# Second MoE of a fused attention and two-MoE kernel: output groups and x steps placed behind a weight pair's seven products

## The chip, the core and the metric

The kernel runs on one core of a Trainium2 chip. The metric is the device time of one execution in microseconds (us). The kernel before has a median of 1036.16 us over 3 runs (1035.74 to 1036.51).

The engines are named as the profile names them: PE is TensorE (matrix products, results go to PSUM), PEld its weight loads, DVE is VectorE, ACT is ScalarE, POOL is GpSimd and SP is SyncE, which here only issues DMAs.

## What is computed

A causal attention with a forget gate, and behind it two feed-forward blocks on 2304 tokens of 512 values. The change touches the second block alone:

```python
def _moe2_ref(x, w_gate, w_val, w_out):          # x 2304x512, w_gate and w_val 512x1536, w_out 1536x512
    gate = 1.0 / (1.0 + np.exp(-(x @ w_gate)))
    val = x @ w_val
    return (gate * val @ w_out).astype(np.float32)
```

## The kernel before, in words

Every float32 product is made of three matmuls on operands split into a high and a low part: high by high, high by low, low by high (function `three`, lines 552 to 558).

The second MoE (class `Moe2`) cuts the tokens into 3 tiles of 768. Within a tile it walks over 12 units: unit r = 0, 2, 4, ... multiplies a pair of column blocks of w_gate, unit r = 1, 3, 5, ... the same pair of w_val, so there are 36 units, k = 0 to 35. One unit computes a 2 by 2 block product with **seven products** instead of eight (a scheme in Strassen's manner), each of 6 matmuls with 384 columns. I call them P1 to P7, in their order in `hidden`: A11, A12, S2, S1, S3, S4, A22.

The seven products share **two PSUM banks**, a and b: P1, P3, P5, P7 go to a, and P2, P4, P6 to b; P3, P5 and P6 add to what the bank already holds. So between two products on one bank the bank has to be read out, and only one product on the other bank lies between. The readers are, each 384 columns wide:

- after P1: ACT copies a to p1 (line 850); after P2: DVE adds b and p1 to c0 (line 853)
- after P3: ACT copies a to u2 (line 856); after P4: ACT copies b to p5 (line 859)
- after P5: ACT copies a to u3 (line 864), and DVE adds a and p5 to c3 (line 865): two readers of one bank, on two engines
- after P6: DVE adds b and u2 to c1 (line 868); after P7: DVE adds a and u3 to c2 (line 876)

In an even unit ACT then applies the sigmoid to c0 and c1 (line 870), and to c2 and c3 in the next unit (line 878). In an odd unit DVE multiplies by the gate (lines 872 and 880), and `high` (line 889, ACT) and `low` (line 895, DVE) split the result.

Beside its seven products a unit carries the **output groups** of a hidden block that was finished two units earlier: six groups (`piece`, lines 914 to 916) of 3 matmuls with 512 columns, which accumulate into six PSUM banks of their own. In the kernel before, the groups lie among the products: one behind each of P3, P4, P5 and P6, and two behind P7 (the calls of `between`). Units 0 and 1 have no output groups. At the end of a tile the six accumulators leave through `leave` (line 925: a copy on DVE or ACT; line 926: a DMA issued by SP); this falls into the unit r = 1 of the next tile and behind the last unit.

In the units r = 2 to 11 of the first two tiles a **step** prepares one tenth of the next tile's x: its DMAs on ACT's queue (line 794), or a split by ACT (line 788) and DVE (line 789) with some subtractions on DVE (lines 799 to 809). It stands behind P4, between the copies to p5 and to u3. Steps for the first tile run in the first MoE, those of the third tile's units don't exist.

The order is written out by hand: the program's order on each engine is the order of the lines. At the end of a unit SP gets the loads of later weights (`load_out`, line 763, and `load`, lines 753 and 758).

Of the kernel before, what the change touches and what calls it, by code (L numbers as in the profile page):

```python
# [551 lines left out]
def three(nc, ps, terms, start, stop, **how):  # L552

    n = len(terms)
    for i, (ah, al, bh, bl) in enumerate(terms):
        nc.tensor.matmul(ps, ah, bh, start=start and i == 0, stop=False, **how)  # L556
        nc.tensor.matmul(ps, ah, bl, start=False, stop=False, **how)  # L557
        nc.tensor.matmul(ps, al, bh, start=False, stop=stop and i == n - 1, **how)  # L558


def block(w, i):
    return w[:, 128 * i:128 * i + 128]


class Moe1:
# [12 lines left out]
    def hidden(self, u, pieces):  # L578
        nc, ch, W = self.nc, self.chain, self.W
        t, fc = divmod(u, self.FC)  # L580
        N = self.TILES[t][1]
        (wh, wl), (xh, xl) = self.W.done[f"wi{fc}"], self.x.parts[t]
        ph = self.ps.tile([128, 512], F32, tag="s", bufs=2, name=f"h{u}")[:, 0:N]
        three(nc, ph, [(block(wh, c), block(wl, c), xh[:, c], xl[:, c]) for c in range(4)], True, True)
        g = ch.tile([128, 512], F32, tag="L", name=f"L{u}", bufs=2)[:, 0:N]
        nc.scalar.activation(g, ph, AF.Softplus)  # L586
        self.mid[u] = g
        self.parts(u)
        W.tick(pieces)
# [38 lines left out]
    def unit(self, u, pieces):  # L628

        t, fc = divmod(u, self.FC)  # L630
        k = fc - 5
        if self.TILES[t][1] < 512:
            k = fc // 2 if fc % 4 in (0, 3) else -1
        if 0 <= k < 8 and t + 1 < self.NT:
            self.x.step(t + 1, k)
        self.hidden(u, pieces)
# [18 lines left out]
class Sums:  # L655
# [11 lines left out]
    def add(self, lane, sums, names, srcs):  # L667

        for n in names:
            self.d[n] = self.dr.tile([4 if sums else 1, 2, 128, 512], F32, name="sd_%s%d" % n)  # L670
        self.lanes[lane].append((sums, names, srcs))
# [52 lines left out]
class Moe2:  # L724
# [95 lines left out]
        return w  # L820


    def hidden(self, k, fill):
        t, r = divmod(k, 2 * self.J)
        nc, gate = self.nc, r % 2 == 0
        m = self.TILES[t][1] // 2
        A, B = self.weights(k), self.tokens(t)
        C = [self.chain("GV"[r % 2] + "01"[f], k) for f in range(2)]
        G = [self.chain("G" + "01"[f], k) for f in range(2)]
        p1, u2, p5, u3 = (self.chain(n, k)[:, 0:m] for n in ("p1", "u2", "p5", "u3"))  # L830
        c = lambda i: C[i // 2][:, m * (i % 2):m * (i % 2) + m]
        if k == 0:
            self.banks = [self.ps.tile([128, 512], F32, tag="s", bufs=2, name=f"z{i}") for i in range(2)]
        a, b = (self.banks[(k + i) % 2][:, 0:m] for i in range(2))

        def product(ps, w, x, start):
            terms = [(block(A[w][0], kk), block(A[w][1], kk), *B[x][kk]) for kk in range(2)]
            three(nc, ps, terms, start, True, skip_group_check=True)

        def issue(fs):  # L840
            while fs:
                fs.pop(0)()

        def between(n=1):
            for _ in range(n):
                if fill:
                    fill.pop(0)()
        add = nc.vector.tensor_add
        product(a, "A11", "x11", True)
        nc.scalar.copy(p1, a)  # L850
        issue(self.early)
        product(b, "A12", "x21", True)
        add(c(0), b, p1)
        issue(self.late)
        product(a, "S2", "T2", False)
        nc.scalar.copy(u2, a)  # L856
        between()
        product(b, "S1", "T1", True)
        nc.scalar.copy(p5, b)
        if t + 1 < self.NT and r >= 2:  # L860
            self.step(t + 1, r - 2)
        between()
        product(a, "S3", "T3", False)
        nc.scalar.copy(u3, a)  # L864
        add(c(3), a, p5)  # L865
        between()
        product(b, "S4", "x22", False)
        add(c(1), b, u2)
        if gate:
            nc.scalar.activation(C[0], C[0], AF.Sigmoid)  # L870
        else:
            nc.vector.tensor_mul(C[0], C[0], G[0])  # L872
            self.high(k // 2, 0, C[0], m)
        between()
        product(a, "A22", "T4", True)
        add(c(2), a, u3)
        if gate:
            self.early.append(lambda: nc.scalar.activation(C[1], C[1], AF.Sigmoid))
        else:
            nc.vector.tensor_mul(C[1], C[1], G[1])  # L880
            self.low(k // 2, 0, C[0], m)
            self.early.append(lambda: self.high(k // 2, 1, C[1], m))
            self.late.append(lambda: self.low(k // 2, 1, C[1], m))
        between(2)

    def high(self, i, f, s, m):
        h = [self.chain(f"gh{x}", i)[:, 0:m] for x in range(2)]
# [38 lines left out]
        nc.sync.dma_start(self.out[o:o + 128, :], z)  # L926

    def unit(self, k, fill):
        self.hidden(k, fill)
        for f in fill:  # L930
            f()
        self.load_out(k + 2)
        self.load()
# [28 lines left out]
def kernel(ctx: ExitStack, tc, q, k, v, f, w_in, w_out, w_gate, w_val, w2_out, out):  # L962
# [60 lines left out]
    for i, (n, j, w) in enumerate(gv):  # L1023
        lane = i % 3 // 2
        unit = lambda: S.add(lane, True, [(n, j)], [w[2 * j], w[2 * j + 1]])
        pair = lambda f: S.add(lane, False, [("w2", f), ("w2", f + 1)], [w2_out[f], w2_out[f + 1]])
        if lane and i < 9:
            pair(4 * (i // 3))
        unit()
        if lane and i < 9:  # L1030
            pair(4 * (i // 3) + 2)
# [118 lines left out]
```

## Time and profile before

| what | value |
|---|---|
| median of 3 runs | 1036.16 us |
| the profiled execution's own time | 1036.21 us |
| its span, first to last instruction | 1034.4 us |
| PE busy in it | 1009.9 us (98%) |
| DVE, ACT, POOL busy | 620.9 (60%), 503.1 (49%), 153.5 (15%) |
| the second MoE's units | 609.5 to 1022 us of the span |

A row of the timeline has the start in us from the span's first instruction, the duration in us, the engine, the line of the code, the operation, out<-in by the program's names and the shape; in brackets stands the idle time of the engine just before it and what ended that. Matmuls are pipelined: one of 384 columns is shown with 0.33 us, yet the next starts 0.17 us after it. What a matmul costs is therefore read from the starts of two neighbours, not from its duration.

The code names p1 and u2 `p` and `u` in the trace; p5 lies in a buffer shown as `bh`, u3 in one shown as `bl`.

### The profile page before, as it was taken

What the parts mean: (1) busy time and instruction counts of PE and PEld (TensorE: products, weight loads), DVE (VectorE), ACT (ScalarE), POOL (GpSimd) and SP (SyncE); (2) the same over time, 40 slices, a digit from 0 to 9 for tenths busy, and PEclk for the clock granted to TensorE, in tenths of its full rate; (3) what the DMA queues carried; (4) which work ended last, traced back from release to release, by engine and by line L of the source; (5) the groups of instructions that cost most, each with busy time, mean ns of one, the idle gap of its engine ahead of it and who ended that gap; (6) DMA issues with size and microseconds to landing.
All of it is one profiled execution on the core that took longest, in us unless ns stands there. A gap on an engine that the chain in (4) does not pass through costs nothing.

```text
span 1034.4 us, 15839 instructions
## 1 busy us (share of the span) xinstructions
PE 1009.9 (98%) x5584; PEld 883.5 (85%) x5584; DVE 620.9 (60%) x1238; ACT 503.1 (49%) x1069; POOL 153.5 (15%) x158
## 2 busy tenths in 40 slices
PE   5999999989999999999999999999999999999998
PEld 4788877768888889988888889999999999999996
DVE  4899999978955666646626743545444434443333
ACT  4889988866544445444334544333333333333332
POOL 8566777540000000000000000000000000000000
PEclk9999999999999999999999999999999999999999
DMA  5354554444635656736525786666667676666631
GB/s 146 111 144 137 157 160 125 138 150 176 217 122 191 221 196 233 255 95 241 195 100 208 252 316 226 208 215 198 224 228 265 203 246 219 207 234 216 223 123 61
DMA packets 114698, 196.07 MB, mean 190 GB/s; under 512 B 14702, under 2 KB 38398, under 8 KB 114620
## 3 DMA queue, kind: packets, MB, share of 16 engines
q1 hardware_dynamic: 112684, 189.98, 55.0%
q10 hardware_dynamic: 1936, 5.09, 1.4%
q8 instruction: 44, 0.72, 0.3%
q14 instruction: 34, 0.28, 0.1%
HBM read 149.19 MB, written 45.83 MB: 189 GB/s over the span
## 4 chain that ended last, share of the span: by engine, by line
PE 91%; DVE 3%; ACT 2%; DMA 1%; issue 1%; SPq 1%; POOL 0%; ACTq 0%; DVEq 0%; POOLq 0%
PE z L558 8%; PE z L557 8%; PE z L556 8%; PE h L556 6%; PE h L557 6%; PE h L558 6%; PE s L223 4%; PE x L330 4%; PE t L254 4%; PE oY L556 2%; PE oY L557 2%; PE oY L558 2%; PE o L557 2%; PE o L558 2%; PE o L556 2%; PE oX L556 2%
## 5 line engine op out<-in xcount | busy, mean ns | idle before, releaser
L557 PE MATMUL z<-three,three 128*128 128x384 f32 x456 | 154.2, 338 | 0.0
L558 PE MATMUL z<-three,three 128*128 128x384 f32 x456 | 153.7, 337 | 0.0
L556 PE MATMUL z<-three,three 128*128 128x384 f32 x456 | 153.0, 336 | 0.5 <-ACT u L856 0.2
L586 ACT ACTIVATE L<-h 128x512 f32<-128x512 f32 (+1 forms) x80 | 44.3, 553 | 152.4 <-PE h L558 152.2
L598 DVE TENSOR_TENSOR gl<-L,gh 128x512 fp32r<-128x512 f32 (+1 forms) x80 | 51.1, 638 | 108.8 <-ACT gh L597 108.6
L556 PEld LDWEIGHTS z<-three,three 128*128 128x128 f32 x456 | 85.6, 188 | 8.1 <-DVE raw L865 0.9
L557 PEld LDWEIGHTS z<-three,three 128*128 128x128 f32 x456 | 85.4, 187 | 6.2
L235 ACT ACTIVATE P<-P,m 128x128 f32<-128x128 f32 (+3 forms) x144 | 83.3, 582 | 10.7 <-DVE m L230 10.3
L558 PEld LDWEIGHTS z<-three,three 128*128 128x128 f32 x456 | 85.7, 188 | 0.0
L230 DVE CUSTOM_DVE_ANT_0 P<-s,mask 128x256 f32<-128x256 f32 (+3 forms) x144 | 70.7, 516 | 12.3 <-PE s L223 7.5
L280 DVE TENSOR_TENSOR PTl<-t,PTh 128x512 fp32r<-128x512 f32 (+2 forms) x112 | 66.9, 619 | 5.1 <-ACT PTh L276 4.9
L254 PE MATMUL t<-ident,P 128*128 128x128 f32 x400 | 61.4, 287 | 7.3 <-DVE PTl L280 5.7
L865 DVE TENSOR_TENSOR raw<-z,bh 128x384 f32<-128x384 f32 x36 | 20.0, 556 | 78.0 <-ACT bl L864 78.0
L276 ACT CAST PTh<-t 128x512 fp32r<-128x512 f32 (+2 forms) x112 | 56.4, 537 | 18.3 <-PE t L254 17.8
L254 PEld LDWEIGHTS t<-ident,P 128*128 128x128 f32 x400 | 44.6, 144 | 21.5 <-DVE PTl L280 7.2
L889 ACT CAST gh<-raw 128x384 fp32r<-128x384 f32 x72 | 33.5, 514 | 50.1 <-DVE raw L872 49.2
L330 PE MATMUL x<-PTh,V 128*128 128x256 f32 (+2 forms) x224 | 56.3, 311 | 0.0
L850 ACT COPY p<-z 128x384 f32<-128x384 f32 x36 | 17.3, 481 | 76.5 <-PE z L558 76.5
L330 PE MATMUL x<-PTl,V 128*128 128x256 f32 (+2 forms) x224 | 54.3, 293 | 0.0
L700 DVE TENSOR_TENSOR l<-fw,sh 128x512 fp32r<-128x512 f32 x60 | 40.7, 687 | 16.2 <-ACT sh L699 14.9
L597 ACT CAST gh<-L 128x512 fp32r<-128x512 f32 (+1 forms) x80 | 46.3, 579 | 2.5
L699 ACT CAST sh<-fw 128x512 fp32r<-128x512 f32 x60 | 35.8, 619 | 19.4 <-DMA sd_g<-sh 9.9
(284 smaller groups left out, 2630.3 us busy)
## 6 DMA issues: line engine op xcount, KB each, us to landing
three<-sd_g SPq DMA_DIRECT2D x126, 256.0 KB
three<-sd_v SPq DMA_DIRECT2D x126, 256.0 KB
two<-sd_w SPq DMA_DIRECT2D x36, 256.0 KB
raw_wi<-in_moe_w_in_dram SPq DMA_DIRECT2D x16, 512.0 KB
raw_wo<-in_moe_w_out_dram SPq DMA_DIRECT2D x16, 512.0 KB
fraw<-in_moe_w_gate_dram SPq DMA_DIRECT2D x12, 512.0 KB
fraw<-in_moe_w_out_dram SPq DMA_DIRECT2D x12, 512.0 KB
sd_g<-sh SPq DMA_DIRECT2D x24, 256.0 KB
```

The costliest lines, as they stand in the source:

```text
L230: self.nc.vector.tensor_tensor_reduce(P, src, mask, -0.125, 3e38, op0=ALU.add, op1=ALU.min, accum_out=R["m"][:, t:t + 1])
L235: self.nc.scalar.activation(P, P, AF.Exp, bias=R["m"][:, t:t + 1], scale=-1.0, accum_out=R["sum"][:, t:t + 1])
L254: nc.tensor.transpose(ps[:, 128 * n:128 * n + 128], R["P"][:, o:o + 128], self.ident)
L276: self.nc.scalar.copy(d, s)
L280: self.nc.vector.tensor_sub(l, s, h)
L330: nc.tensor.matmul(R["acc%d" % h][:, o:o + n], v, t[:, col:col + n], start=j == 0 and w == 0, stop=j == 1 and w == 1)
L556: nc.tensor.matmul(ps, ah, bh, start=start and i == 0, stop=False, **how)
L557: nc.tensor.matmul(ps, ah, bl, start=False, stop=False, **how)
L558: nc.tensor.matmul(ps, al, bh, start=False, stop=stop and i == n - 1, **how)
L586: nc.scalar.activation(g, ph, AF.Softplus)
L597: nc.scalar.copy(gh, s)
L598: nc.vector.tensor_sub(gl, s, gh)
```

## The change

`hidden` loses its argument `fill` and with it the calls of `between`: P1 to P7 now follow each other in the program with their readers alone. The x step moves from behind P4 to the end of `hidden`. The six output groups are emitted by `unit`, behind `hidden`. Nothing is added or removed, and the order of P1 to P7, of their readers and of the groups among themselves stays.

```diff
-    def hidden(self, k, fill):
+    def hidden(self, k):
...
-        def between(n=1):
-            for _ in range(n):
-                if fill:
-                    fill.pop(0)()
...
         product(a, "S2", "T2", False)
         nc.scalar.copy(u2, a)
-        between()
         product(b, "S1", "T1", True)
         nc.scalar.copy(p5, b)
-        if t + 1 < self.NT and r >= 2:
-            self.step(t + 1, r - 2)
-        between()
         product(a, "S3", "T3", False)
         nc.scalar.copy(u3, a)
         add(c(3), a, p5)
-        between()
         product(b, "S4", "x22", False)
         add(c(1), b, u2)
...
-        between()
         product(a, "A22", "T4", True)
         add(c(2), a, u3)
...
-        between(2)
+        if t + 1 < self.NT and r >= 2:
+            self.step(t + 1, r - 2)
...
     def unit(self, k, fill):
-        self.hidden(k, fill)
+        self.hidden(k)
         for f in fill:
             f()
```

## Rows read from the trace of the kernel before

**Rows 1.** The page, parts 1 and 2: busy time, and the granted clock in 40 slices

```profile
PE 1009.9 (98%) x5584; PEld 883.5 (85%) x5584; DVE 620.9 (60%) x1238; ACT 503.1 (49%) x1069; POOL 153.5 (15%) x158
PEclk9999999999999999999999999999999999999999
```

**Rows 2.** By stretch: length, busy PE, PEld, DVE, ACT, POOL, clock, DMA: unit 1; twelve units

```profile
619.97:628.27 8.30, 7.90 (x43) 7.25 (x42) 2.89 (x5) 3.22 (x7) 0.00 (x0) 1.00 0.65 223
778.44:917.08 138.64, 138.64 (x721) 128.95 (x720) 61.38 (x103) 49.86 (x95) 0.00 (x0) 1.00 0.68 229
```

**Rows 3.** Timeline of PE: unit 3's P1, first group and P4; unit 35's P1

```profile
639.82 0.33 PE L556 MATMUL z<-three,three 128*128 128x384 f32 x1
...
642.94 0.39 PE L914 MATMUL zt<-raw,gh 128*128 128x512 f32 x1
...
643.64 0.33 PE L556 MATMUL z<-three,three 128*128 128x384 f32 x1
...
1009.64 0.33 PE L556 MATMUL z<-three,three 128*128 128x384 f32 x1
```

**Rows 4.** Timeline of unit 34: P5's last matmul and its two readers

```profile
1004.56 0.33 PE L558 MATMUL z<-three,three 128*128 128x384 f32 x1
...
1004.98 0.48 ACT L864 COPY bl<-z 128x384 f32<-128x384 f32 x1 [1.28 <-PE z L558]
...
1005.50 0.56 DVE L865 TENSOR_TENSOR raw<-z,bh 128x384 f32<-128x384 f32 x1 [3.57 <-ACT bl L864]
```

**Rows 5.** Line 865's own view: what ended the idle time before it (us, times)

```profile
  ACT bl L864: 78.0, 24
```

**Rows 6.** Timeline of PE, unit 0: starts of P1, P6, P7, the next matmuls, unit 1

```profile
609.48 0.33 PE L556 MATMUL z<-three,three 128*128 128x384 f32 x1
...
614.74 0.33 PE L556 MATMUL z<-three,three 128*128 128x384 f32 x1
...
616.06 0.44 PE L556 MATMUL z<-three,three 128*128 128x384 f32 x1
...
617.21 0.39 PE L556 MATMUL oX<-gh,wo_h 128*128 128x512 f32 x1
...
619.97 0.33 PE L556 MATMUL z<-three,three 128*128 128x384 f32 x1
```

**Rows 7.** Timeline of unit 1: P6, the two readers of P5, P7, unit 2's P1

```profile
625.73 0.33 PE L556 MATMUL z<-three,three 128*128 128x384 f32 x1
...
625.98 0.48 ACT L864 COPY bl<-z 128x384 f32<-128x384 f32 x1 [1.08 <-PE z L558]
...
626.50 0.56 DVE L865 TENSOR_TENSOR raw<-z,bh 128x384 f32<-128x384 f32 x1 [3.00 <-ACT bl L864]
...
627.11 0.44 PE L556 MATMUL z<-three,three 128*128 128x384 f32 x1 [0.17 <-DVE raw L865]
...
628.27 0.33 PE L556 MATMUL z<-three,three 128*128 128x384 f32 x1
```

**Rows 8.** Timeline of PE behind the last unit: the output groups at the end

```profile
1021.42 0.40 PE L915 MATMUL zt<-three,gh 128*128 128x512 f32 x1
1022.08 0.50 PE L916 MATMUL zt<-three,gl 128*128 128x512 f32 x1 [0.26 <-DVE gl L895]
1022.41 0.40 PE L914 MATMUL zt<-three,gh 128*128 128x512 f32 x1
...
1029.46 0.39 PE L915 MATMUL zY<-two,gh 128*128 128x512 f32 x1
```

**Rows 9.** Timeline of DVE: unit 8 (c0, x step), unit 14 (last DVE leave, c0)

```profile
699.92 0.56 DVE L853 TENSOR_TENSOR bl<-z,p 128x384 f32<-128x384 f32 x1 [1.05 <-PE z L558]
...
703.96 0.96 DVE L789 TENSOR_TENSOR three<-bh,three 128x768 fp32r<-128x768 f32 x1 [2.54 <-ACT three L788]
...
768.40 0.69 DVE L925 COPY fw<-zY 128x512 f32<-128x512 f32 x1
769.24 0.56 DVE L853 TENSOR_TENSOR bl<-z,p 128x384 f32<-128x384 f32 x1 [0.15 <-PE z L558]
```

## The prediction, made before the changed kernel was run

> **What bounds the kernel now.** I read the page first: PE is busy for 98% of the span at the full granted clock, and POOL has nothing to do in the second half [rows 1]. Then the busy time by stretch: in twelve units of the second MoE PE is busy for all of 138.64 us, while DVE and ACT work for 44% and 36% of it, and the clock is at 1.00, the level of 2.4 GHz [rows 2]. So PE's stream is the bound, and the other engines count only where PE would have to wait for them. Third, the timeline of PE: from unit 3's P1 to unit 35's P1 lie 32 units in 369.82 us, **11.557 us a unit** [rows 3]. Three products one behind the other take 642.94 - 639.82 = 3.12 us, so 1.04 us a product, and an output group between two products takes 0.70 us [rows 3]. PE never stops in these units.
>
> The decisive view is the timeline around P5. Its last matmul starts at 1004.56; ACT starts the u3 copy 0.42 us later and takes 0.48 us; DVE's c3 add, which needs only the bank and the older p5, starts at 1005.50, 0.04 us behind the end of the copy, and takes 0.56 us [rows 4]. The add waited for the copy in all 24 of the 36 units in which DVE was otherwise free [rows 5]. So the two readers of bank a go one behind the other, and P7, which overwrites that bank, can start about 0.42 + 0.48 + 0.04 + 0.56 + 0.05 = 1.55 us after P5's last matmul did. Now P6 and two groups lie in between (0.17 + 1.04 + 2 x 0.70 = 2.6 us), which hides it.
>
> Units 0 and 1 have no output groups: the trace of before already holds **the order that the change makes**, seven products back to back. There PE does stop. In unit 0 P6 starts at 614.74 and P7 at 616.06, 1.32 us instead of 1.04 to 1.05; in unit 1 it is 627.11 - 625.73 = 1.38 us, and the row of P7 names line 865 as its releaser [rows 6, 7].
>
> **Part 1, the products close up.** P1 to P5 of unit 0 take 614.74 - 609.48 = 5.26 us, with no wait of any size [rows 6]; so one product is enough cover for the readers of P1 to P4, which are single (0.42 + 0.48 + 0.05 = 0.95 us for a copy on ACT, 1.03 us for an add on DVE, against 0.17 + 1.04 = 1.21 us). That cover is thin, 0.2 us. P6 up to P7 takes 1.32 us in unit 0 and 1.38 us in unit 1; I take the 1.38 us, since there the copy starts as late as in the later units (0.42 us after P5's last matmul, as in rows 4 and 7). P7 itself takes longer behind the stop: 617.21 - 616.06 = 1.15 us and 628.27 - 627.11 = 1.16 us [rows 6, 7]. Sum of the seven products: 5.26 + 1.38 + 1.16 = **7.80 us**.
>
> **Part 2, the six groups in one piece.** Eighteen matmuls of 512 columns behind a product: twelve of the first MoE's take 619.97 - 617.21 = 2.76 us [rows 6], and deep in such a run they follow at (1029.46 - 1022.41) / 31 = 0.227 us [rows 8], so 2.76 + 6 x 0.227 = **4.12 us**. That is less than six single groups (6 x 0.70 = 4.20 us); the products gain a little too where no group interrupts them, and both are in these sums.
>
> A unit becomes 7.80 + 4.12 = 11.92 us against 11.557 us: **+0.36 us in each of the 34 units with groups (2 to 35)**, +12.3 us. The banks' readers after P6 and P7 lie under the groups then, so the next unit's P1 and P2 find them done.
>
> **Part 3, the end.** Behind the last unit PE now stops for the split that the last groups need: from 1021.42 to 1022.41 pass 0.99 us for two matmuls instead of 0.45, released by line 895 on DVE [rows 8]. With four more groups (2.8 us) between P7 and these, that split is done in time: **-0.5 us**.
>
> **Part 4, the x step.** Twenty steps move. Of each, ACT's copy of 768 columns and DVE's 0.96 us subtraction [rows 9] with at most two of 384 columns behind it (0.56 us each, by the add of that width in rows 4) leave the place between p5 and u3 and come behind P7's readers. In unit 8 the step ran ahead of c3; that cost nothing, and its absence gains nothing, as c3 is tied to u3. Behind it on DVE now stands the next unit's c0, which P4 waits for. In unit 8 DVE stood idle for 1.05 us before c0 with no DVE step in the unit before [rows 9]; four groups more behind P7 add 2.8 us to that, a step takes about 2.1 us from it, so some 1.7 us remain: no cost. The step's two DMA issues (units r = 2 and r = 7) move on ACT's queue past u3 and the sigmoid; the data is used a unit later, as before. SP's loads stay behind the last group of the unit, which still ends the unit; POOL has no part in it. Cost nothing, as long as those 1.7 us hold.
>
> **Part 5, the accumulators' leaving (units 13 and 25).** The copies of line 925 now come within 4 us, and the fifth must find the buffer of the first sent out. In unit 14 DVE had only 0.15 us to spare between such a copy and c0 [rows 9]. After the change the last DVE copy ends about as close to c0. I take nothing for it; the bound is that each of the two copies ends one copy later, 0.69 us [rows 9], so 0 to +1.4 us.
>
> **Sum.** +12.3 - 0.5 = +11.8 us; of this I take 0.1 off for units 14 and 26, the first of their tiles, which like unit 0 should wait 0.06 us less. On the profiled execution's own 1036.21 us that gives **1047.9 us**; the median before is 1036.16 us, so nothing changes between the two bases. Bounds: with unit 0's shorter wait everywhere and P1 without the 0.02 us that it costs behind a long run of groups, 11.83 us or +0.27 us a unit, 34 x 0.27 - 0.5 = +8.7, 1044.9 us; with part 5's 1.4 us and a few tenths where the 0.2 us covers fail by chance, 1049.9 us.
>
> **The rivals.** *Faster: c3 is not tied to u3.* If DVE reads the bank beside ACT, P7 can start 0.42 + 0.56 + 0.05 = 1.03 us after P5's last matmul, and the cover of 1.21 us holds. A unit then takes 6.30 + 1.04 + 4.12 = 11.46 us, 0.10 us less than now: 34 x 0.10 + 0.5 = 3.9 us saved, **1032.3 us**. For it: neither reader needs the other's result. Against it: all 24 free cases, and both units without groups [rows 5 to 7]; the program's order of these two lines stays. Of the Trainium skill two pages bear on this one. "TensorE: Matmul & The Clock Gate" (Loop structure matters more than you think) recommends matmuls back to back, with the copy out of PSUM beside them and the next matmuls following at once; by it the time would be this rival's. "PSUM — Partial Sum Buffer" (PSUM bank collisions raise a hardware error) says that two engines must not touch one bank at a time, two reads included, and wants a semaphore there; by that rule the tie stays, and the 24 waits agree.
>
> *Slower still: the moved step delays c0.* If DVE's step runs into the next unit's c0 by d, P4 starts late by about d - 0.2 us. It decides once the step ends over 1.7 us later than I have it, for instance because a DMA of x lands late; then 20 units with 0.3 us each, **1054 us**. Against it: DVE's share of 44% [rows 2].
>
> *No change: the tie is there, but closing up repays it.* That needs 0.36 us a unit found elsewhere; the groups and products have no more to give than the sums hold. It would be 1036 us, or 1034.1 to 1038.3 us, the 0.2% within which a measurement of this kernel can't tell a change.
>
> **How the numbers follow.** My forecast 0.87, the faster rival 0.07, the slower one 0.04, no change 0.02. The likeliest case gives 1047.9 us; its bounds 1044.9 to 1049.9 hold over 8 in 10, and the others stay outside. Faster by over 0.2%: 0.07; within: 0.02; slower: 0.91.
>
> **What would show it.** In the changed trace each unit from 2 on should have one stop of PE, ahead of P7, released by line 865's add, with P6 to P7 at about 1.38 us; the c3 add should start within 0.05 us of u3's end; the unit should take 11.92 us, its 18 group matmuls 4.12 us; the stop behind the last unit should be gone. I am wrong if the add starts beside the copy, if P7 starts 1.04 us after P6, or if a stop ahead of P4 or of the next P1 appears.

## The result, and the profile after

| | before | after |
|---|---|---|
| median | 1036.07 us (1035.74 to 1036.51, 4 runs) | 1048.02 us (1047.70 to 1048.62, 4 runs) |
| ratio to before | | 1.0119, 95% interval 1.0106 to 1.0131 |
| profiled execution, its span | 1036.21 us, 1034.4 us | 1048.24 us, 1046.5 us |

The changed kernel is 1.2% slower; 1047.9 us was predicted. The lines of the code have moved: the copy to u3 is now line 856 (864 before), the c3 add line 857 (865), c1 859 (868), c0 849 (853), the output groups 905 to 907 (914 to 916).

The page of the changed kernel, to be held against [rows 1]; the third row is the group of the first matmuls of `three` (after the bar: busy us, mean ns; after the second bar: idle us before them, and what ended most of it), and the fourth is the same group in the kernel before:

```profile
PE 1017.3 (97%) x5584; PEld 884.1 (84%) x5584; DVE 619.1 (59%) x1238; ACT 503.1 (48%) x1069; POOL 152.8 (15%) x158
PEclk9999999989999999999999999999999999999999
L556 PE MATMUL z<-three,three 128*128 128x384 f32 x456 | 157.6, 346 | 6.4 <-DVE raw L857 6.0
...
L556 PE MATMUL z<-three,three 128*128 128x384 f32 x456 | 153.0, 336 | 0.5 <-ACT u L856 0.2
```

PE has the same 5584 matmuls. New is the idle time ahead of line 556, 6.4 us where it was 0.5, 6.0 us of it released by the c3 add. That is only half of the loss: a matmul is drawn with 0.33 us though the next could start after 0.17, so a part of each stop lies under the drawn end of the matmul before it. Again the starts of neighbours are what counts. The one slice with a clock of 8 lies at 209 to 235 us, in the attention, and is not where the time went: unit 0's P1 starts at 609.36 us, and at 609.48 us before [rows 6].

The timeline of unit 34 in the changed kernel: P5's last matmul, P6, u3, c3, P6's last matmul, P7, the first group, unit 35's P1. The first row of all is unit 3's P1:

```profile
640.22 0.33 PE L556 MATMUL z<-three,three 128*128 128x384 f32 x1
...
1015.04 0.33 PE L558 MATMUL z<-three,three 128*128 128x384 f32 x1
1015.21 0.34 PE L556 MATMUL z<-three,three 128*128 128x384 f32 x1
...
1015.47 0.48 ACT L856 COPY bl<-z 128x384 f32<-128x384 f32 x1 [0.56 <-PE z L558]
...
1015.98 0.56 DVE L857 TENSOR_TENSOR raw<-z,bh 128x384 f32<-128x384 f32 x1 [2.16 <-ACT bl L856]
...
1016.08 0.34 PE L558 MATMUL z<-three,three 128*128 128x384 f32 x1
...
1016.59 0.45 PE L556 MATMUL z<-three,three 128*128 128x384 f32 x1 [0.17 <-DVE raw L857]
...
1017.77 0.39 PE L905 MATMUL zt<-two,gh 128*128 128x512 f32 x1
...
1021.89 0.33 PE L556 MATMUL z<-three,three 128*128 128x384 f32 x1
```

Read it against [rows 4]. P5's last matmul starts at 1015.04; u3 follows 0.43 us later, c3 0.03 us behind u3's end, P7 0.05 us behind c3's end: 1016.59 - 1015.04 = 1.55 us. Between P6's first matmul and P7's lie 1.38 us instead of 1.04. P7 takes 1.18 us, the 18 group matmuls 1021.89 - 1017.77 = 4.12 us. From unit 3 to unit 35 lie (1021.89 - 640.22) / 32 = **11.927 us a unit**, against 11.557 us before [rows 3]: 0.37 us each.

The views of line 857 (what it waited for and who waited for it: us, times) and of PE's waits (engine, line, us in total, times, longest) in the changed kernel from 600 us on give the same on all units; the third fence is PE's waits in the kernel before:

```profile
  ACT bl L856: 95.1, 36
...
  PEld z L556: 17.7, 36
```

```profile
PE z L556 <- DVE raw L857: 6.0, 35, 0.2
PE z L556 <- ACT u L852: 0.2, 1, 0.2
```

```profile
PE zt L916 <- DVE gl L895: 0.3, 1, 0.3
PE z L556 <- ACT u L856: 0.2, 1, 0.2
PE z L556 <- DVE raw L865: 0.2, 1, 0.2
```

c3 waited for u3 in all 36 units (24 in [rows 5]; in the others the x step had kept DVE busy), and weight loads waited for c3 in all 36. The stop behind the last unit [rows 8], released by line 895 then, has no row any more.

### The profile page after: what moved, and what is told of

Same layout as the page of the kernel before. It is cut to its first block, busy times and chain, and to the rows that moved or that the text cites. A ratio compares the mean times of both kernels' runs of the same rounds, so it can differ in the third digit from the quotient of the medians.

```text
span 1046.5 us, 15854 instructions
## 1 busy us (share of the span) xinstructions
PE 1017.3 (97%) x5584; PEld 884.1 (84%) x5584; DVE 619.1 (59%) x1238; ACT 503.1 (48%) x1069; POOL 152.8 (15%) x158
## 4 chain that ended last, share of the span: by engine, by line
PE 89%; DVE 6%; ACT 3%; issue 1%; DMA 1%; ACTq 0%; SPq 0%; DVEq 0%
PE z L556 8%; PE z L558 7%; PE z L557 7%; PE h L557 6%; PE h L558 6%; PE h L556 6%; PE s L223 5%; PE x L330 4%; PE t L254 4%; PE oY L557 2%; PE oY L556 2%; PE oY L558 2%; PE o L557 2%; PE o L558 2%; PE o L556 2%; DVE raw L857 2%
## 5 line engine op out<-in xcount | busy, mean ns | idle before, releaser
L849 DVE TENSOR_TENSOR raw<-z,p 128x384 f32<-128x384 f32 x18 | 10.0, 558 | 88.9 <-PE z L558 88.9
```

## Experiments

The theory: the two readers of bank a after P5, on two engines, go one behind the other; this chain of 1.55 us needs more than one product as cover, and with the groups gone from between the products PE stops ahead of P7 in every unit. Rivals: the moved x step costs the time; the order itself does (long stretches of one shape); or c3 waits for something of u3's own and not for the bank's other reader.

### The step put back, the groups alone behind

```diff
         nc.scalar.copy(p5, b)
+        if t + 1 < self.NT and r >= 2:
+            self.step(t + 1, r - 2)
         product(a, "S3", "T3", False)
...
-        if t + 1 < self.NT and r >= 2:
-            self.step(t + 1, r - 2)
```

> The changed kernel with the x step put back between the copies to p5 and to u3; only the output groups lie behind the products. Theory (PE stops ahead of P7 because c3 must follow u3 on bank a): the step's DVE work now stands ahead of c3 with no group to cover it. In the units of the first two tiles where c3 came late in the trace of before (4 units with p5's start to c3's start 3.2 us, 8 units with 2.6 us), P7 moves later by 1.6 and 1.05 us: 4 x 1.6 + 8 x 1.05 = 15 us over the changed kernel, so about 1063 us (1060 to 1066), with the longer stop in these 12 units alone. Rival (the moved step is what costs the 12 us): with the step back in its place the time returns, 1036 to 1040 us.

Measured: **1067.62 us**, ratio 1.0306 (1.0292 to 1.0320). Slower still, so the moved step is not what costs; left in place it would have cost some 20 us more. The timelines of DVE and PE in unit 8 of this kernel (c3 is line 859 here), then PE's waits:

```profile
708.65 0.96 DVE L789 TENSOR_TENSOR three<-bh,three 128x768 fp32r<-128x768 f32 x1 [1.85 <-ACT three L788]
709.52 0.55 DVE L799 TENSOR_TENSOR bl<-bh 128x384 f32<-128x384 f32 x1
710.11 0.56 DVE L800 TENSOR_TENSOR bh<-bh 128x384 f32<-128x384 f32 x1
710.59 0.55 DVE L859 TENSOR_TENSOR raw<-z,bh 128x384 f32<-128x384 f32 x1
```

```profile
709.06 0.34 PE L558 MATMUL z<-three,three 128*128 128x384 f32 x1
711.20 0.45 PE L556 MATMUL z<-three,three 128*128 128x384 f32 x1 [1.80 <-DVE raw L859]
...
712.12 0.52 PE L557 MATMUL z<-three,three 128*128 128x384 f32 x1
712.43 0.52 PE L558 MATMUL z<-three,three 128*128 128x384 f32 x1
```

```profile
PE z L556 <- DVE raw L859: 20.9, 34, 1.8
```

The step's three DVE instructions stand ahead of c3 in DVE's order, and P7 starts 2.14 us after P6's last matmul instead of 0.17. That is the expected part. The result lies 1.6 us above the expected range, and the rows show why: behind the stop two matmuls of 384 columns lie 0.31 us apart, not 0.17. The busy time by stretch in this kernel (length, busy time and count of PE, PEld, DVE, ACT, POOL, then the granted clock) for unit 3, the end of unit 8 and unit 4, whose stop is shorter:

```profile
639.73:653.25 13.52, 11.72 (x61) 10.65 (x60) 6.85 (x11) 4.22 (x8) 0.00 (x0) 1.00 0.52 176
...
711.20:716.00 4.80, 4.80 (x15) 4.11 (x16) 0.96 (x2) 0.84 (x1) 0.00 (x0) 0.64 0.06 19
...
653.25:666.18 12.93, 11.73 (x61) 10.66 (x60) 4.41 (x8) 4.22 (x8) 0.00 (x0) 1.00 0.55 182
```

After the stop of unit 8 the granted clock falls to its lower level of 1.2 GHz for a while (0.64 as the mean of the stretch). Units 15 and 20 show the same (0.89 as the mean of each unit), unit 3 doesn't, though its stop is as long. These three units take 15.1 us against unit 3's 13.52 us: 3 x 1.6 = 4.8 us, which brings the expected 1063 us to 1067.8 (the profiled execution took 1066.82 us).

### The step alone moved

```diff
         nc.scalar.copy(p5, b)
-        if t + 1 < self.NT and r >= 2:
-            self.step(t + 1, r - 2)
         between()
...
         between(2)
+        if t + 1 < self.NT and r >= 2:
+            self.step(t + 1, r - 2)
```

> The kernel before with the x step alone moved behind P7's readers; the groups stay among the products. Theory: the step is off the path in either place, 1036.1 us (1035.5 to 1036.7), units of 11.55 us, c3 right behind u3 in every unit. Rival (the moved step delays the next unit's c0, or its DMAs come late): 1038 us or more, with a stop ahead of P4.

Measured: **1035.71 us**, ratio 0.9995 (0.9985 to 1.0004): no change. PE is busy for all of 360 us in this kernel's busy time by stretch, although the step now runs right up to the next unit's c0 on DVE (no idle time ahead of line 853 in the second fence):

```profile
640.00:1000.00 360.00, 360.00 (x1872) 334.60 (x1871) 152.02 (x256) 125.56 (x242) 0.00 (x0) 1.00 0.65 221
```

```profile
653.57 0.56 DVE L800 TENSOR_TENSOR bh<-bh 128x384 f32<-128x384 f32 x1
654.05 0.55 DVE L853 TENSOR_TENSOR bl<-z,p 128x384 f32<-128x384 f32 x1
```

In this order a group stands between P3 and P4 and covers c0: c0 ends at 654.60, P4 starts at 654.72, and the group starts at 654.02, where P4 would have stood without it. So the step costs nothing here, but because of the group and not because DVE had time to spare.

### One reader of the bank: c3 made from u3

```diff
         nc.scalar.copy(u3, a)
-        add(c(3), a, p5)
+        add(c(3), u3, p5)
```

> The changed kernel with c3 made from u3, the copy in SBUF of what bank a holds, and not from bank a: the same sum, but bank a has one reader after P5. Theory (the two readers one behind the other are the whole loss): P7 can start about 0.42 + 0.48 + 0.05 = 0.95 us after P5's last matmul, the cover is 1.21 us, so the stop goes: units of 11.46 us, 34 x 0.47 less than the changed kernel, about 1032 us (1031 to 1033.5), faster than both. Rival (runs of one shape, seven products and six groups at a stretch, cost by themselves, or another wait takes the place of this one): 1040 to 1048 us.

Measured: **1030.91 us**, ratio to the kernel before 0.9948 (0.9935 to 0.9960): faster than both kernels, with one word changed. The timeline of its unit 34 (P5's last matmul, u3, c3, P7) between its unit 3's and unit 35's P1:

```profile
638.00 0.33 PE L556 MATMUL z<-three,three 128*128 128x384 f32 x1
...
997.56 0.33 PE L558 MATMUL z<-three,three 128*128 128x384 f32 x1
...
997.98 0.48 ACT L856 COPY bl<-z 128x384 f32<-128x384 f32 x1 [0.56 <-PE z L558]
...
998.50 0.56 DVE L857 TENSOR_TENSOR raw<-bl,bh 128x384 f32<-128x384 f32 x1 [2.15 <-ACT bl L856]
...
998.77 0.33 PE L556 MATMUL z<-three,three 128*128 128x384 f32 x1
...
1003.93 0.33 PE L556 MATMUL z<-three,three 128*128 128x384 f32 x1
```

c3 still starts at u3's end, but now it reads `bl`, that is u3, and P7 starts while it runs: 998.77 - 997.56 = 1.21 us, the plain length of the cover. No stop of PE is left in units 3 to 35. A unit takes (1003.93 - 638.00) / 32 = 11.435 us, 0.49 us less than in the changed kernel and 0.12 us less than before. So the order as such is a small gain; the stop turned it into the loss.

### The same edit in the old order

```diff
         nc.scalar.copy(u3, a)
-        add(c(3), a, p5)
+        add(c(3), u3, p5)
         between()
```

> The kernel before with c3 made from u3 in the same way; groups and step stay where they were. Theory: a group between P5 and P6 and another between P6 and P7 hide the two readers anyway, so nothing changes: 1036.1 us (1035.4 to 1036.7). Rival (taking a read off the PSUM bank helps PE, DVE or ACT by itself, whatever the order): 1034 us or less.

Measured: **1035.73 us**, ratio 0.9995 (0.9987 to 1.0004): no change. Where the groups stand among the products, the second reader is hidden anyway, and units take 11.55 us as before. The edit is worth something only where the cover is short: units 0 and 1, which have no groups, lose their stop and take 10.07 and 7.82 us instead of 10.49 and 8.30 us. Unit 2 gives 0.3 us of that back, and the rest is too little to show in the median.

### One group put back, between P6 and P7

```diff
         else:
             nc.vector.tensor_mul(C[0], C[0], G[0])
             self.high(k // 2, 0, C[0], m)
+        if fill:
+            fill.pop(0)()
         product(a, "A22", "T4", True)
```

(`unit` hands `fill` to `hidden` again; the five other groups stay behind.)

> The changed kernel with one of the six output groups put back, between P6 and P7; the other five and the step stay behind, and c3 still reads bank a. Theory: u3 and c3 one behind the other need 1.55 us from P5's last matmul to P7, and P6 with one group covers 0.17 + 1.04 + 0.70 = 1.91 us, so this one group takes the whole stop away: units of about 11.51 us (7.31 for the products, 4.12 for the groups, 0.08 for the two further changes of shape), 1033.5 us (1032.5 to 1034.8), below the kernel before, above the one in which c3 reads u3. Rival (it takes groups behind every product, or the long stretch of groups, to get the time back): 1036 us or more, stops left.

Measured: **1033.88 us**, ratio 0.9982 (0.9974 to 0.9991). One group of 0.70 us in the right place takes the whole stop away, and c3 still reads the bank. The timeline of unit 9: its P1, c3, the group, P7, and unit 10's P1:

```profile
707.86 0.33 PE L556 MATMUL z<-three,three 128*128 128x384 f32 x1
...
713.88 0.56 DVE L857 TENSOR_TENSOR raw<-z,bh 128x384 f32<-128x384 f32 x1 [3.09 <-ACT bl L856]
...
714.16 0.39 PE L907 MATMUL zt<-two,gh 128*128 128x512 f32 x1
...
714.86 0.33 PE L556 MATMUL z<-three,three 128*128 128x384 f32 x1
...
719.36 0.33 PE L556 MATMUL z<-three,three 128*128 128x384 f32 x1
```

c3 ends at 714.44, 0.42 us ahead of P7. A unit takes 11.50 us (11.52 us in the mean from unit 3's P1 to unit 35's), as expected. The mean is higher because units 14, 15, 16 and 26 take 11.60 to 11.78 us. In 14 and 26, behind a tile's end, the last DVE copy of the accumulators (line 918 here) waited 1.6 us for a DMA to free its buffer, c0 comes right behind it, and P4 is held up. The DVE rows of unit 14:

```profile
767.36 0.69 DVE L918 COPY fw<-zY 128x512 f32<-128x512 f32 x1 [1.59 <-DMA out_dram<-fw]
767.97 0.55 DVE L849 TENSOR_TENSOR bl<-z,p 128x384 f32<-128x384 f32 x1
```

### The two readers exchanged

```diff
-        nc.scalar.copy(u3, a)
         add(c(3), a, p5)
+        nc.scalar.copy(u3, a)
```

> The changed kernel with the two readers of bank a exchanged: the c3 add on DVE first, the u3 copy on ACT behind it. Theory (any two engines that read this bank go one behind the other, in the program's order): now the copy starts when the add has ended, P7 comes 0.42 + 0.56 + 0.04 + 0.48 + 0.05 = 1.55 us after P5's last matmul, and the time is that of the changed kernel, 1047.5 us (1046.5 to 1048.6). Rival (c3 waits for something of u3's own, its buffer or ACT's order, and not for the other reader of the bank): both readers start together, P7 comes 1.03 to 1.1 us after P5's last matmul, 1032 us.

Measured: **1048.30 us**, ratio 1.0124 (1.0110 to 1.0138), the time of the changed kernel. Here c3 is line 856 and u3 line 857; the timeline of unit 6 (P5's last matmul, c3, u3, P7):

```profile
680.68 0.33 PE L558 MATMUL z<-three,three 128*128 128x384 f32 x1
...
681.12 0.56 DVE L856 TENSOR_TENSOR raw<-z,bh 128x384 f32<-128x384 f32 x1 [1.66 <-PE z L558]
...
681.72 0.48 ACT L857 COPY bl<-z 128x384 f32<-128x384 f32 x1 [1.18 <-DVE raw L856]
...
682.25 0.44 PE L556 MATMUL z<-three,three 128*128 128x384 f32 x1 [0.19 <-ACT bl L857]
```

Now the copy waits for the add, which it needs for nothing; P7 comes 1.57 us after P5's last matmul. So the tie is between two readers of one bank, in the program's order, and belongs neither to u3's buffer nor to ACT. The profile infers a releaser from semaphore events, so what it shows is a wait that stands in the built program; whether the chip itself would hold the second reader back is not shown. Whether two reads at once would do harm can't be tried without taking the wait itself away, and was not tried. The Trainium skill, "PSUM — Partial Sum Buffer" (PSUM bank collisions raise a hardware error), says that two engines on one bank have to be kept apart, two reads included; the order seen here agrees with that.

### The add made twice

```diff
         nc.scalar.copy(u3, a)
         add(c(3), a, p5)
+        add(c(3), a, p5)
```

> The changed kernel with the c3 add made twice, one behind the other, which changes no value. Theory: the second add lies on the path from P5 to P7 in every unit, and DVE starts two such adds 0.47 to 0.56 us apart, so every stop ahead of P7 grows by that: 36 units x 0.47 to 0.56, 1065 to 1068 us. At 0.8 to 0.9 us a stop I expect no change of the clock (stops of 1.37 us left it at 2.4 GHz in the kernel with the step put back, stops of 1.96 us brought it down in three of four units). Rival (the lost time is not a path through c3 but a price of the order): within 2 us of the changed kernel, 1048 to 1050 us.

Measured: **1069.88 us**, ratio 1.0333 (1.0317 to 1.0349). Each of the 36 units is longer by (1069.88 - 1048.02) / 36 = 0.61 us; the whole added instruction lies on the path. The expected range ended at 1068: the timeline of unit 34 (the two adds are lines 857 and 858) shows a step of 0.59 us between them, not 0.47 to 0.56: the second add, which writes what the first wrote, starts 0.03 us behind its end. The DVE rows of unit 8 with the step put back agree: line 800, which overwrites what line 799 reads, comes 0.59 us after it, and c3, which shares nothing with line 800, 0.48 us after that.

```profile
1036.50 0.56 DVE L857 TENSOR_TENSOR raw<-z,bh 128x384 f32<-128x384 f32 x1 [2.16 <-ACT bl L856]
...
1037.09 0.56 DVE L858 TENSOR_TENSOR raw<-z,bh 128x384 f32<-128x384 f32 x1
...
1037.70 0.44 PE L556 MATMUL z<-three,three 128*128 128x384 f32 x1 [0.77 <-DVE raw L858]
```

36 x 0.59 = 21 us. The clock stayed at 2.4 GHz through these stops (1.00 as the mean from 630 to 1030 us), as expected.

## Why the prediction was right

**What bounds the kernel, and units 0 and 1 as a preview.** Right. The two units without groups ran the new order in the trace of before, and unit 1's 1.38 us from P6 to P7 [rows 7] is what the later units of the changed kernel take (1.37 or 1.38 us in each). Two readings were too smooth. Unit 1 has a second stop, ahead of P5 (P4 to P5 takes 1.43 us there), which the prediction passes over: u2's copy stood behind a copy of the first MoE on ACT. It does not come back in the later units, so leaving it out did no harm. And PE does lose a little in one of the 32 units in which it "never stops": unit 27 takes 11.69 us, 0.14 us more than its neighbours.

**Part 1, the products.** Right in the sum: predicted 7.80 us; unit 34's P1 starts at 1009.96 in the same timeline, its groups at 1017.77, which makes 7.81 us. The single readers are covered by one product, as said: in the later units c0 ends some 0.2 us ahead of P4 and u2 some 0.3 us ahead of P5. P4 takes about 0.03 us longer than its neighbours in most units, although no reader holds it up; why is open, and unit 0's 5.26 us held as much.

**Part 2, the groups.** Right: 4.12 us predicted, 4.12 us measured. That closing up is itself a gain, 0.12 us a unit, only the run with c3 from u3 shows in the open.

**Part 3, the end.** Right: the stop behind the last unit is gone. From unit 35's P1 to the end of the span lie 1046.5 - 1021.89 = 24.6 us instead of 1034.4 - 1009.64 = 24.8 us, although the unit itself is 0.37 us longer: 0.5 us.

**Part 4, the step.** Right: nothing lost, and the run with the step alone moved bears it out. The spare time on DVE ahead of c0 was put at 1.7 us; the least behind a step with DVE work is the 1.88 us in this first row of the changed kernel's DVE timeline:

```profile
654.50 0.56 DVE L849 TENSOR_TENSOR bl<-z,p 128x384 f32<-128x384 f32 x1 [1.88 <-PE z L558]
...
772.77 0.69 DVE L916 COPY fw<-zY 128x512 f32<-128x512 f32 x1 [1.58 <-PE z L558]
773.80 0.56 DVE L849 TENSOR_TENSOR bl<-z,p 128x384 f32<-128x384 f32 x1 [0.34 <-PE z L558]
```

What the prediction missed about the step is that its move is not neutral in the new order but needed: in its old place it would have cost another 20 us. "Its absence gains nothing" holds for the old order only.

**Part 5, the accumulators' leaving.** Right to take nothing: the last DVE copy ends 0.34 us ahead of c0 (the two further rows), and units 14 and 26 are no longer than others. The margin is thin: with one group put back the copy did wait for its buffer, the risk that this part named, and units 14 and 26 take 0.2 us more than the others.

**The sum.** Two small terms were off, both in the same direction. Units 14 and 26 were to wait 0.06 us less, like unit 0; they wait like the others, 11.93 us. And unit 2, which follows unit 1 without groups between, has a short stop ahead of its own P4, as DVE is still at unit 1's gating; it takes 640.22 - 628.13 = 12.09 us, 0.16 us more than the mean (628.13 is its P1 in the changed kernel's timeline). By the prediction's own last list a stop ahead of P4 was to be a sign of error; it came in this one unit alone. That the second MoE starts 0.14 us earlier than before (unit 2's P1 at 628.13, at 628.27 in [rows 7]) about makes up for unit 2. 34 x 0.37 = 12.6, less 0.5: 12.1 us, the difference of the spans (1046.5 - 1034.4).

The prediction's own difference was 11.7 us and that of the medians is 11.95 us. So the mechanism and the large terms are right; that the time is met within 0.1 us is partly luck, since the base of 1036.21 us lies 0.14 us above the median of the kernel before.

**The rivals.** That c3 isn't tied to u3 was the one on the other side; exchanging the readers shows the tie from both ends, and taking it away gives 1030.9 us, close to the 1032.3 us that this rival was priced at. The price was good, its condition false. The recommendation cited for it, matmuls back to back with the copy out of PSUM beside them (the Trainium skill, "TensorE: Matmul & The Clock Gate", Loop structure matters more than you think), cost 0.37 us a unit here while bank a had two readers one behind the other, and gained 0.12 us a unit once each bank's read-out fitted beside one product. The slower rival and that of no change did not occur.

## What to carry to other kernels

Before work is moved out from between products that share PSUM banks, add up the readers of each bank between two products as a chain (start after the last matmul, each reader, each hand-over), since the two engines that read one bank here went one behind the other in all 36 units, in either order; compare it with what stays between the products. If the chain is longer, shorten it first: let the second reader take the copy that the first has made (one word here: 1030.9 us in place of 1048.0, 0.5% below the kernel before), or leave a single group in the one place that needs it. And look for units that lack the work to be moved: they show the new order in the old trace.

## What the runs showed of the hardware beyond that

With the step put back, PE sat idle for 1.8 us ahead of P7 in four units and was busy around that; in three of the four the granted clock then fell from 2.4 to 1.2 GHz, which cost 1.6 us each, nearly as much again as the stop. Why unit 3 was spared is open. Idle times of 0.8 us (the add made twice) and of 1.2 us (units 4 and 5 with the step put back, 1.00 in each; unit 4 is the last row of the clock above) left it alone. I had expected a stop to cost its own length and 0.1 us.

Groups of 0.70 us among products of 384 columns make a unit of 11.55 us, the same matmuls in two stretches 11.435 us. From these two figures I estimate about 0.03 us for each of the four places where a group between two products has gone. Units 29, 31 and 33 of the run with one group put back agree: with one such place they take 11.46 to 11.47 us. That it is the change of shape that costs this is argued and not shown.
